# Sparse attention and a top-2 mixture of experts on one core: the eight zero fills of the output at other places in the program

## The chip, the core and the metric

The kernel runs on one core of one Trainium2 chip. The metric is the device time of one execution in microseconds (us), the median of the runs. Five engines work side by side, each with its own queue of instructions: TensorE (PE in the profile; PEld is its weight load), VectorE (DVE), ScalarE (ACT), GpSimd (POOL) and SyncE (SP). SP issues nearly all transfers between the chip's memory (DRAM) and the on-chip memory (SBUF); they run on the core's 16 DMA engines, which all queues share. GpSimd issues the gathers and scatters by row number.

## The reference

Four batches of eight heads, 768 positions, 64 wide. Attention is block-sparse with blocks of 32: a block sees itself, its neighbours, the first and the last block, and three sampled ones; the first and last block see everything.

```
scores = where(mask, q @ k.T / 8, -1e9); attn = softmax(scores); x = attn @ v   # -> 3072 rows of 512
logits = x @ w_gate + log1p(exp(x @ w_noise)) * noise
top2, top2_w = the two largest of 8 experts, softmax over the two
out = zeros((3072, 512)); for e, k: out[rows] += top2_w * (relu(x[rows] @ w1[e]) @ w2[e])
```

The output starts as zeros, since the experts add to it row by row. Those zeros are what the change is about.

## The kernel before, in words

The first part is attention. It is a chain of 64 items, 16 for each batch, walked by `Attention.steps`. Twelve items of a batch are tiles of 128 query rows, `("q", b, t, f)` with tile t of six and half f of the heads; four are the global blocks, `("g", ...)`. Step k writes out the scores of item k+2 (line 264), the transposes of item k (line 331), and the product with the values of item k-1 (line 359), so three items are in work at once. The order of all instructions is the order in which this Python code writes them (`manual_schedule`); each engine takes its own in that order.

SP's queue is filled by the same steps. For a tile it carries q (line 195), the near rows of the values (`va`, line 227) and the three sampled blocks for each 32 rows (`va` and `vb`, line 232). A tile's values come in two halves of seven transfers; in batch four there are two buffers for them instead of three, so that a tile's loads wait until the product of two tiles before has freed its buffer. From the early steps of batches one to three SP also carries the next batch's keys (`kk`, line 172), which GpSimd scales (line 184) and then copies, block by block, to `kc` (lines 204 and 205). Finished rows go to DRAM as `x_rows` (line 636). Each transfer of SP also waits for the completion of the one issued eight places earlier, since eight completion counters are used in turn.

`step(n, 3)` at the end of step n runs what the table `plan` holds for n. Before, this is a memset of `spare()` by GpSimd at step 49 (a part of the buffer `xs[2]`, free by then) and `fill_out(i)` for i = 0 to 7 at steps 49, 50, 51, 52, 54, 55, 56 and 57. One `fill_out` sets 384 rows of the output to zero: a DMA of 768 pieces of 1 KB, 786,432 bytes, out of one zeroed row of 256 floats in each partition. Fills 4 to 7 read the zeroed part of `xg`, which exists from step 53 on. In the same stretch the table loads the first expert's weights (`wraw`, line 905), and from step 59 on gathers the first expert's rows (line 998) and transposes them by DMA (`xta`, line 1008).

The second part are ten units of expert work (lines 1056, 1095, 1142 on TensorE). The first scatter to the output is issued at 352.1 us. After the last unit comes a branch for rows beyond the fixed capacity.

Of the kernel before, what the change touches and what calls it, by code (L numbers as in the profile page):

```python
# [9 lines left out]
F32 = mybir.dt.float32  # L10
# [10 lines left out]
P = 128  # L21
# [7 lines left out]
C = 816  # L29
# [19 lines left out]
class Attention:  # L49
# [25 lines left out]
    def open(self, ctx, early, ident):  # L75
        tc, nc = self.tc, self.nc
        pool = lambda c, name, bufs, **kw: c.enter_context(tc.tile_pool(name=name, bufs=bufs, **kw))
        self.const = pool(ctx, "aconst", 1, side="right")
        self.buf = pool(ctx, "abuf", 1, side="right")
        self.qp = pool(ctx, "aq", 3, side="right")  # L80
        self.pp = pool(ctx, "app", 2, side="right")
        self.gp = pool(early, "agp", 3)
        self.sm = pool(ctx, "asm", 4, side="right")
        self.xp = pool(ctx, "axp", 2, side="right")
        self.ps_s = pool(ctx, "ps_s", 3, space=PSUM)
        self.ps_o = pool(ctx, "ps_o", 2, space=PSUM)
        ep = pool(early, "aeb", 1)
        two = lambda n: ep if n == 2 else self.buf
        J = self.NJ
        self.va = [two(i).tile([P, J, self.HW], F32, name=f"va{i}") for i in range(3)]  # L90
        self.vb = [two(i).tile([P, J, self.HW], F32, name=f"vb{i}") for i in range(3)]
        self.kk = [two(2 - 2 * i).tile([P, self.NB, P], F32, name=f"kk{i}") for i in range(2)]
        self.kc = [self.buf.tile([P, J, self.NP, 8, 32], F32, name=f"kc{i}") for i in range(2)]
        self.qgt = [two(2 - 2 * i).tile([P, self.NP, 64], F32, name=f"qg{i}") for i in range(2)]
        self.ends = [two(2).tile([P, self.HD], F32, name=f"ends{i}") for i in range(2)]
        self.xs = [self.buf.tile([P, self.NP, 2, P], F16, name=f"x{n}") for n in range(2)]
        self.og = self.const.tile([P, 4, self.W], F32, name="og")
        self.known = self.const.tile([P, self.NB, 2], F32, name="known")
        self.pgt = [self.buf.tile([P, 8, P], F32, name=f"pgt{i}") for i in range(4)]
        self.ident = ident  # L100
        self.ident16 = self.const.tile([P, P], F16, name="a_ident16")
        nc.vector.tensor_copy(self.ident16, self.ident)
        nc.vector.memset(self.known, 1.0 / XS)

    def open_x(self, ctx):
        p = ctx.enter_context(self.tc.tile_pool(name="axs", bufs=1))
        self.xs += [p.tile([P, self.NP, 2, P], F16, name=f"x{n}") for n in (2, 3)]
# [1188 lines left out]
def kernel(ctx, tc, qt, qg, kt, vx0, vx1, vx2, vx3, vw, vg, sampled_blocks, gates, noise, w1, w2, out):  # L1296
    nc = tc.nc
# [9 lines left out]
    ex = Experts(tc, router, w1, w2, out, x_dram)  # L1307
    att = Attention(tc, qt, qg, kt, (vx0, vx1, vx2, vx3), vw, vg, sampled_blocks, H, DM // H)
# [16 lines left out]
    PER = NS // att.B  # L1325
    EC = PER * 3 + 5
    UB = 9

    def spare():
        return att.xs[2].rearrange("p n a c -> p (n a c)")[:, 0:512].bitcast(F32)  # L1330

    def fill_out(i):
        z = spare() if i < 4 else ex.xg[:, C // P, 0:512].bitcast(F32)
        nc.sync.dma_start(out[i * 384:(i + 1) * 384].rearrange("(p n) (h d) -> p (n h) d", p=P, d=256),
                          z[:, None, :].to_broadcast([P, 3 * DM // 256, 256]))

    plan = {}
    at = lambda n, f, *a: plan.setdefault(n, []).append((f, a))

    def gather_early(c):  # L1340
        ex.gather(0, c)

    at(PER * 3 + 1, lambda: nc.gpsimd.memset(spare(), 0.0))
    for i in range(8):
        at(PER * 3 + 1 + i + i // 4, fill_out, i)
    for i in range(3):
        at(EC + 1 + i, ex.load_piece, 0, i)
    at(NS - 4, ex.split_piece, 0, 0)
# [162 lines left out]
    for u in range(nu):  # L1511
        left_ = ex.rows(u)[1]
        n = ex.count(u)
# [64 lines left out]
```

## Time and profile before

| what | value |
|---|---|
| median of 3 runs | 862.2 us (859.36 to 864.88) |
| profiled execution | 858.13 us, its span 856.3 us |
| mean granted TensorE clock | 0.964 of full |
| TensorE busy | 793.2 us, 93% of the span |
| attention, first to last product | up to about 312 us |
| DMA traffic | 148.86 MB |

The profile is one execution. A row of the timeline gives the start, the length, the engine, the source line and the operation, and in brackets how long the engine stood idle before it and what ended that. SPq is SP's queue: its length is that of issuing, not of the transfer. In a table of windows the first numbers are the stretch and its length, then the busy time of PE, PEld, DVE, ACT and POOL with the number of instructions, then PEclk (the granted TensorE clock as a share of full), the mean busy share of the DMA engines (it can pass 1 a little) and GB/s.

### The profile page before, as it was taken

The numbers are of one execution on the slowest core, as the hardware profiler recorded it, in microseconds if no ns is written. First come the engines' busy times: TensorE is split into PE (matmuls) and PEld (weight loads), VectorE is DVE, ScalarE is ACT, GpSimd is POOL, SyncE is SP. The second block draws the span as 40 slices with busy tenths as digits, with TensorE's granted clock in tenths as the row PEclk, the third lists the DMA queues.
The fourth block names the chain that finished last, engine by engine and source line by source line (L and its number), as shares of the span: only waits on it lengthen the run. The fifth ranks groups of instructions, "written<-read, shape, count | busy, mean of one in ns | idle before, by whom it ended". The sixth has DMA issues, their size and how long they took to land.

```text
span 856.3 us, 24921 instructions
## 1 busy us (share of the span) xinstructions
PE 793.2 (93%) x9799; PEld 489.4 (57%) x9799; DVE 582.9 (68%) x1160; ACT 400.5 (47%) x736; POOL 380.7 (44%) x656
## 2 busy tenths in 40 slices
PE   7899899988877869999997989999999999999996
PEld 4666576666546647466585544554554554554553
DVE  6765697788687418752528698697697696796631
ACT  5869758858634325322114542552542632633510
POOL 5773587577564230130615426426336335322311
PEclk8999999999978769999999999999999999999999
DMA  7666786685869976650977939639539549523301
GB/s 232 205 189 175 203 234 184 202 237 168 270 192 268 235 182 160 205 181 9 210 169 164 207 122 237 190 100 238 174 111 235 170 115 232 165 90 108 103 29 52
DMA packets 119840, 148.86 MB, mean 174 GB/s; under 512 B 69515, under 2 KB 76300, under 8 KB 119714
## 3 DMA queue, kind: packets, MB, share of 16 engines
q1 hardware_dynamic: 107490, 109.22, 48.3%
q0 software_dynamic: 12224, 37.96, 13.9%
q8 instruction: 79, 1.29, 0.7%
q14 instruction: 47, 0.39, 0.2%
HBM read 107.28 MB, written 26.15 MB: 156 GB/s over the span
## 4 chain that ended last, share of the span: by engine, by line
PE 72%; DVE 10%; DMA 6%; ACT 6%; issue 3%; SPq 2%; POOL 0%; POOLq 0%; DVEq 0%; ACTq 0%
PE pc L1142 28%; PE pa L1095 10%; PE ps L264 5%; PE po L359 5%; PE pd L1095 5%; PE pa L1056 4%; PE ps L331 4%; PE pc L1095 3%; PE pd L1056 2%; PE pc L1151 2%; PE po L382 2%; ACT p L304 2%; DMA va<-in_vx_dram 2%; DVE m L301 2%; DMA va<-in_vw_dram 1%
## 5 line engine op out<-in xcount | busy, mean ns | idle before, releaser
L1142 PE MATMUL pc<-w,hh 128*128 128x512 f16 x768 | 228.4, 379 | 0.0
L1175 POOL DMA_INDIRECT out_dram<-y,r_xT x46 | 64.2, 1395 | 218.4 <-DVE y L1174 179.0
L1095 PEld LDWEIGHTS <-w 128*128 128x128 f16 x1008 | 99.1, 98 | 82.7 <-issue 7.9
L1142 PE MATMUL pc<-w,hl 128*128 128x512 f16 x384 | 145.5, 379 | 0.0
L1142 PEld LDWEIGHTS <-hh 128*128 128x128 f16 x768 | 74.6, 98 | 86.4
L304 ACT ACTIVATE p<-ps,m 128x256 f32<-128x256 f32 x192 | 75.1, 476 | 57.7 <-DVE m L301 51.1
L204 POOL COPY kc<-kk 128x128 f32 x264 | 69.5, 300 | 26.6 <-PE ps L264 19.0
L359 PE MATMUL po<-va,ptr 128*32 128x68 f32 x1536 | 60.7, 235 | 17.4 <-DMA va<-in_vx_dram 9.3
L301 DVE TENSOR_REDUCE m<-ps 128x4 f32<-128x1024 f32 x48 | 58.6, 1221 | 25.1 <-PE ps L264 24.8
L998 POOL DMA_INDIRECT xg<-x_rows,r_xT x46 | 61.5, 1337 | 14.7 <-issue 14.7
L944 DVE SCALAR_TENSOR_TENSOR w<-wraw,w 128x1024 f16<-128x1024 f32 (+1 forms) x58 | 64.2, 1110 | 0.8 <-ACT w L940 0.8
L264 PE MATMUL ps<-kc,q 64*32 64x256 f32 x1536 | 57.4, 408 | 7.4 <-ACT pgt L319 3.1
L1142 PEld LDWEIGHTS <-hl 128*128 128x128 f16 x384 | 37.6, 98 | 45.3
L1016 POOL DMA_INDIRECT pv<-out_dram,r_xT x44 | 49.8, 1132 | 28.5 <-issue 25.0
L359 PE MATMUL po<-vb,ptr 128*32 128x68 f32 x1536 | 58.0, 232 | 2.4 <-issue 1.4
L1095 PE MATMUL pa<-tb,w 128*128 128x408 f16 x288 | 56.6, 340 | 3.8 <-ACT ta L1083 3.8
L359 PEld LDWEIGHTS po<-va,ptr 128*32 128x32 f32 x1536 | 42.3, 114 | 29.6 <-issue 11.0
L940 ACT ACTIVATE w<-wraw 128x1024 f16<-128x1024 f32 (+1 forms) x58 | 55.7, 960 | 5.8 <-DMA wraw<-in_moe_w_dram 5.8
L1095 PE MATMUL pd<-tb,w 128*128 128x408 f16 x288 | 56.5, 336 | 1.9 <-ACT tc L1083 1.9
L1174 DVE SCALAR_TENSOR_TENSOR y<-pc,r_xT,pv 128x512 f32<-128x512 f32 x37 | 27.7, 750 | 43.6 <-PE pc L1142 43.6
L331 PE MATMUL ps<-r_ident,p 128*128 128x128 f32 x384 | 56.5, 292 | 0.5 <-issue 0.5
L1064 ACT ACTIVATE hh<-pa 128x408 f16<-128x408 f32 (+2 forms) x56 | 24.2, 442 | 66.0 <-PE pa L1056 53.9
(239 smaller groups left out, 1544.4 us busy)
## 6 DMA issues: line engine op xcount, KB each, us to landing
wraw<-in_moe_w_dram SPq DMA_DIRECT2D x64, 512.0 KB, 3.9
va<-in_vw_dram SPq DMA_DIRECT2D x40, 384.0 KB, 5.0
vb<-in_vx_dram SPq DMA_DIRECT2D x176, 64.0 KB, 3.6
q<-in_qt_dram SPq DMA_DIRECT2D x24, 256.0 KB, 3.7
va<-in_vx_dram SPq DMA_DIRECT2D x88, 64.0 KB, 4.2
kk<-in_kt_dram SPq DMA_DIRECT2D x18, 256.0 KB, 4.0
x_rows<-x SPq DMA_DIRECT2D x16, 256.0 KB, 3.5
out_dram<-x SPq DMA_DIRECT2D x4, 768.0 KB, 7.3
```

The lines of the kernel that those rows point to most:

```text
L204: nc.gpsimd.tensor_copy(kc[:, j, :, 3 + n], flat[:, bass.ds(self.listed(blk, n), P)].rearrange("p (n c) -> p n c", c=32))
L264: mm = lambda o, l, r: nc.tensor.matmul(o, l, r, start=True, stop=True, skip_group_check=True)
L301: nc.vector.tensor_reduce(m, s.rearrange("p a (e c) -> p a e c", e=2), axis=AX.X, op=ALU.max, negate=True)
L304: i = nc.scalar.activation(p[:, 2 * e + par], s[:, par, 256 * e:256 * e + 256], AF.Exp, bias=m[:, par, e:e + 1])
L331: self.apart(it, par, nc.tensor.transpose(t[:, e, c], p[:, 2 * e + par, P * c:P * c + P], self.ident))
L359: nc.tensor.matmul(o[32 * j:32 * j + 32, h], d[:, h % 2, h // 2, x, 32 * j:32 * j + 32], self.values(v[:, self.slot(t, j)], 4 * f + h), st ...
L940: self.nc.scalar.activation(hi, t, AF.Copy, scale=WS)
L944: self.nc.vector.scalar_tensor_tensor(lo, t, WS, hi, op0=ALU.mult, op1=ALU.subtract)
L998: nc.gpsimd.indirect_dma_start(out=self.xg[0:m, c + self.place(u)], out_offset=None, in_=self.x_dram[0:nr], in_offset=bass.IndirectOffsetO ...
L1095: nc.tensor.matmul(o, w[:, wt, slot, s * P:s * P + P], mv(s, a), start=i == 0 and p in tail, stop=i == 5, skip_group_check=True)
L1142: nc.tensor.matmul(py, h[:, f, o], w(f)[:, x], start=i == 0, stop=i == last)
L1175: d = nc.gpsimd.indirect_dma_start(out=self.out, out_offset=bass.IndirectOffsetOnAxis(ap=r["ix"][0:m, c:c + 1], axis=0), in_=y[0:m], in_of ...
```

## The change

The zeros of fills 0 to 3 come from a tile of their own, `zero`, of 1 KB in each partition, which VectorE sets once at the start; the memset of `spare()` on GpSimd is gone. Fills 0 and 1 move to steps 18 and 27 (batch two), fills 2 and 3 to steps 34 and 43 (batch three). Fills 4 to 7 go from steps 54, 55, 56, 57 to steps 54, 56, 58, 60.

```diff
@@ Attention.open
         nc.vector.memset(self.known, 1.0 / XS)
+        self.zero = self.const.tile([P, 256], F32, name="zero")
+        nc.vector.memset(self.zero, 0.0)
@@ kernel
-    def spare():
-        return att.xs[2].rearrange("p n a c -> p (n a c)")[:, 0:512].bitcast(F32)
-
     def fill_out(i):
-        z = spare() if i < 4 else ex.xg[:, C // P, 0:512].bitcast(F32)
+        z = att.zero if i < 4 else ex.xg[:, C // P, 0:512].bitcast(F32)
@@
-    at(PER * 3 + 1, lambda: nc.gpsimd.memset(spare(), 0.0))
-    for i in range(8):
-        at(PER * 3 + 1 + i + i // 4, fill_out, i)
+    for i in range(4):
+        at(PER * (1 + i // 2) + 9 * (i % 2) + 2, fill_out, i)
+        at(PER * 3 + 6 + 2 * i, fill_out, 4 + i)
```

The order on TensorE and ScalarE stays as it was; VectorE gains one row, GpSimd loses one. What moves is SP's queue. First, its rows at step 18, the start of batch two, where the second tile's values are followed by the next batch's keys, a q tile and two stores; before:

```order
L232 DMA vb_101<-in_vx_dram 32x2048 x2
L172 DMA kk_102<-in_kt_dram 128x512 x2
L195 DMA q<-in_qt_dram 128x512
L636 DMA x_rows<-xe 128x1024 x2
L172 DMA kk_102<-in_kt_dram 128x512
L177 DMA qg_106<-in_qg_dram 128x256
```

and now:

```order
L234 DMA vb_101<-in_vx_dram 32x2048 x2
L174 DMA kk_102<-in_kt_dram 128x512
L1333 DMA out_dram<-zero 768x1x256
L174 DMA kk_102<-in_kt_dram 128x512
L197 DMA q<-in_qt_dram 128x512
L638 DMA x_rows<-xe 128x1024 x2
L174 DMA kk_102<-in_kt_dram 128x512
```

Fill 0 stands between the first and the second load of the keys, ahead of q; fill 2 stands in the same way at step 34, the start of batch three. Fill 1 and fill 3 stand behind the last half of a batch's values, ahead of a q tile or a store.

Second, SP's rows in batch four from the second half of tile 2 to the first half of tile 3; before:

```order
L227 DMA va_96<-in_vw_dram 96x2x512
L232 DMA va_96<-in_vx_dram 32x2048
L232 DMA vb_99<-in_vx_dram 32x2048 x2
L232 DMA va_96<-in_vx_dram 32x2048
L232 DMA vb_99<-in_vx_dram 32x2048 x2
L1334 DMA out_dram<-xg 768x1x256
L905 DMA wraw<-in_moe_w_dram 128x1024
L227 DMA va_97<-in_vw_dram 96x2x512
```

and now:

```order
L229 DMA va_96<-in_vw_dram 96x2x512
L234 DMA va_96<-in_vx_dram 32x2048
L234 DMA vb_99<-in_vx_dram 32x2048 x2
L234 DMA va_96<-in_vx_dram 32x2048
L234 DMA vb_99<-in_vx_dram 32x2048 x2
L907 DMA wraw<-in_moe_w_dram 128x1024
L229 DMA va_97<-in_vw_dram 96x2x512
```

One fill has gone from ahead of tile 3; it comes after that half instead, where the third one stood.

Third, SP's rows at the end of batch four, the two halves of its last tile; before:

```order
L227 DMA va_97<-in_vw_dram 96x2x512
L232 DMA va_97<-in_vx_dram 32x2048
L232 DMA vb_100<-in_vx_dram 32x2048 x2
L232 DMA va_97<-in_vx_dram 32x2048
L232 DMA vb_100<-in_vx_dram 32x2048 x2
L1008 DMA_TRANSPOSE xta<-xg 128x8x128 x2
L227 DMA va_97<-in_vw_dram 96x512
L232 DMA va_97<-in_vx_dram 32x2048
```

and now:

```order
L229 DMA va_97<-in_vw_dram 96x2x512
L234 DMA va_97<-in_vx_dram 32x2048
L234 DMA vb_100<-in_vx_dram 32x2048 x2
L234 DMA va_97<-in_vx_dram 32x2048
L234 DMA vb_100<-in_vx_dram 32x2048 x2
L1333 DMA out_dram<-xg 768x1x256
L1010 DMA_TRANSPOSE xta<-xg 128x8x128 x2
L229 DMA va_97<-in_vw_dram 96x512
L234 DMA va_97<-in_vx_dram 32x2048
```

The eighth fill stands between the two halves of the last tile's values now. Counted along this queue, four fills stand ahead of that last half from the start of batch four's tile 2 on, before and now; ahead of tile 3's second half there were three and are two.

## Rows read from the trace of the kernel before

**Rows 1.** The page's second part: 40 equal slices of 21.4 us, in tenths.

```profile
PEclk8999999999978769999999999999999999999999
DMA  7666786685869976650977939639539549523301
```

**Rows 2.** Windows: stretch, busy time by engine, granted clock, DMA share, GB/s.

```profile
106.00:110.00 4.00, 2.27 (x42) 1.35 (x44) 3.13 (x9) 1.63 (x6) 3.17 (x11) 0.75 1.01 345
...
174.00:178.00 4.00, 2.95 (x98) 2.22 (x98) 2.52 (x8) 2.35 (x8) 4.00 (x16) 1.00 1.01 299
...
132.00:142.00 10.00, 9.66 (x224) 7.02 (x224) 6.58 (x14) 8.71 (x18) 8.23 (x22) 1.00 0.62 191
...
202.00:212.00 10.00, 8.86 (x197) 6.29 (x192) 6.55 (x16) 9.53 (x20) 7.53 (x22) 1.00 0.53 159
226.00:238.00 12.00, 9.18 (x156) 5.91 (x154) 6.52 (x14) 8.18 (x18) 4.30 (x14) 0.86 1.00 335
238.00:246.00 8.00, 4.24 (x133) 3.41 (x127) 7.39 (x35) 2.67 (x7) 6.25 (x18) 0.91 0.22 69
246.00:262.00 16.00, 13.06 (x257) 9.71 (x254) 14.89 (x38) 6.20 (x15) 8.26 (x19) 0.72 0.84 260
262.00:302.00 40.00, 30.52 (x705) 23.18 (x703) 21.92 (x53) 17.50 (x38) 15.13 (x30) 0.83 0.97 247
```

**Rows 3.** SP's timeline where batches two and three begin.

```profile
101.97 1.80 SPq L172 DMA_DIRECT2D kk<-in_kt_dram  x2
103.87 0.37 SPq L195 DMA_DIRECT2D q<-in_qt_dram  x1
...
169.81 1.30 SPq L195 DMA_DIRECT2D q<-in_qt_dram  x1
```

**Rows 4.** Tile q in the stretch 101 to 104.5: from issue to landing.

```profile
DMA to landing us min/median/max: 3.7/3.7/3.7
```

**Rows 5.** GpSimd's timeline at the same places.

```profile
105.56 0.62 POOL L184 TENSOR_SCALAR kk<-kk 128x512 f32<-128x512 f32 x1 [5.37 <-DMA kk<-in_kt_dram]
107.00 0.62 POOL L184 TENSOR_SCALAR kk<-kk 128x512 f32<-128x512 f32 x1 [0.83 <-DMA kk<-in_kt_dram]
...
172.78 1.27 POOL L184 TENSOR_SCALAR kk<-kk 128x512 f32<-128x512 f32 x2 [3.88 <-DMA kk<-in_kt_dram]
```

**Rows 6.** TensorE's timeline at the same places.

```profile
107.73 1.75 PE L264 MATMUL ps<-kc,q 64*32 64x256 f32 x32 [2.58 <-POOL kk L184]
...
174.15 1.10 PE L264 MATMUL ps<-kc,q 64*32 64x256 f32 x32 [0.28 <-ACT p L304]
...
179.07 0.26 PE L359 MATMUL po<-va,ptr 128*32 128x68 f32 x3 [1.76 <-issue]
```

**Rows 7.** The chain that ended last, in batch four: the three longest transfers in it.

```profile
269.05 7.11 DMA va<-in_vx_dram
...
289.46 6.01 DMA va<-in_vw_dram
...
299.06 3.29 DMA vb<-in_vx_dram
```

**Rows 8.** Who waited for whom on TensorE, 215 to 312 us: total, times, longest.

```profile
PE po L359 <- DMA va<-in_vx_dram: 8.5, 4, 3.2
```

**Rows 9.** TensorE's transposes in batch four, ahead of a stall and behind it.

```profile
269.14 1.09 PE L331 MATMUL ps<-r_ident,p 128*128 128x128 f32 x8
...
278.83 1.97 PE L331 MATMUL ps<-r_ident,p 128*128 128x128 f32 x8
```

**Rows 10.** SP's timeline: two fills in batch four.

```profile
249.71 0.55 SPq L1334 DMA_DIRECT2D out_dram<-xg  x1
...
257.80 0.55 SPq L1334 DMA_DIRECT2D out_dram<-xg  x1
```

**Rows 11.** VectorE's timeline: its first wait, and a memset of 256 floats.

```profile
2.00 0.18 DVE L123 CAST rf<-sb 1x72 f32<-1x72 int32 x1 [0.39 <-DMA sb<-in_sampled_blocks_dram]
...
11.96 0.27 DVE L602 MEMSET r_acc<- 128x256 f32 x1
```

## The prediction

> **What bounds the kernel now.** I read the page's slices first, to see where the transfers are dense and where TensorE's clock falls; then windows of the DMA share over the places that a fill leaves or enters; then, at those places, the timelines of SP, GpSimd and TensorE, and the chain.
>
> The slices show two things in the attention part, slices 1 to 15 [rows 1]: the DMA engines are never idle for long, and the only deep dip of TensorE's clock (down to 0.6) lies in slices 12 to 15, about 236 to 321 us, which is the end of batch four. The windows split that up [rows 2]. From 226 to 238 us the engines are full (1.00, 335 GB/s): that is where fills 0 to 3 run. From 238 to 246 they are nearly empty (0.22), because the next values wait for a buffer that TensorE frees. From 246 to 262 they are at 0.84, from 262 to 302 at 0.97. In this last stretch the transfers set the pace: the chain goes through three long ones, 7.11, 6.01 and 3.29 us [rows 7], and TensorE's products with the values wait 8.5 us for them in four stalls [rows 8].
>
> Batches two and three look otherwise: there the chain is work on the engines, with one weak spot each, the start of the batch. At 101.97 SP gets to the next keys late; GpSimd waits 5.37 us for them [rows 3, 5], and TensorE's scores of tile 3 start at 107.73 after 2.58 us of idleness [rows 6]. The row names GpSimd's second scaling, which ended at 107.62; the q tile of these scores was issued at 103.87 and took 3.7 us [rows 3, 4], so it landed at 107.57. Both releasers come from SP's queue at the same spot, and a fill ahead of them delays both.
>
> **The change part by part.** Prices first. One fill is 786,432 bytes. At the 335 GB/s of the stretch in which fills and little else ran it takes 2.35 us, at the 247 GB/s of the full end of batch four 3.2 us [rows 2]; at the 299 GB/s of a full stretch in batch three 2.6 us, which I take, as it is the nearest place. SP issues one in 0.55 us when nothing holds it up [rows 10].
>
> *The new zero tile.* VectorE's memset of 256 floats takes 0.27 us; its first wait, for the sampled blocks, is 0.39 us, and the memset stands ahead of it [rows 11]. Cost 0. GpSimd loses a memset of the same size that nobody waited for: 0.
>
> *Fills 0 to 3 leave batch four.* They ran from 226 to 238 in front of 8 us of nearly idle DMA engines [rows 2], and no engine waits for a transfer there. The next values start when a buffer is free, not when the fills are through. So the gain is 0, and by the same idle stretch it cannot be more than the little that two q tiles behind the fills come earlier.
>
> *Fill 0, step 18.* It stands between the two loads of the keys, ahead of the q tile that tile 3's scores wait for. There is no slack: TensorE idles until that tile is there. Cost 2.6 us; the lower bound is 0, if the fill, which only writes, runs beside the loads, which only read; the upper is 3.2 + 0.55 = 3.75 us. The Trainium skill, "DMA: Bandwidth & Descriptors", section "Queues, rings and completion order", says that on each DMA engine the descriptors of one queue are consumed in ring order. By that rule the q tile waits for the whole fill, as in the value taken, and the lower bound falls away; no row here shows a load that is waited for right behind a fill alone.
>
> *Fill 2, step 34.* The same place in batch three. Here the scores start at 174.15 after 0.28 us of idleness that ended with ScalarE [rows 6]. The q tile was issued from 169.81 to 171.11 [rows 3]; with the 3.7 us of the other one [rows 4], counted from the start of the issue, it landed at 173.5, and at the latest it landed at 174.15. So the slack is at most 0.7 us, and GpSimd waits 3.88 us for the keys as before [rows 5]. Of 2.6 us some 2.2 would come through. But 3 us later TensorE idles 1.76 us for nothing that the profile shows [rows 6], in a window in which the DMA engines are full (1.01) [rows 2]; if what it lacks then arrives during the new stall, part of that goes. I take 1.5, with bounds of 0 and 3.75.
>
> *Fills 1 and 3, steps 27 and 43.* They go to stretches of 10 us in which the DMA engines stand at 0.62 and 0.53, which leaves 3.8 and 4.7 us for 2.6 [rows 2]. Cover: those gaps. Cost 0; without the cover at most the two issues, 1.1 us.
>
> *Fills 4 to 7, later in batch four.* Two effects of opposite sign. Tile 3's second half has one fill less ahead of it, so the first long stall should shrink by up to 2.6 us. But the stall that ends last is that of the last tile's last half (3.29 us of the chain), and ahead of that stand the same four fills, the same values and the same gathers. In a stretch at 0.97 the same bytes take the same time; what is gained early is lost behind the eighth fill. The time that can be won is what the engines were idle: 0.16 of 16 us and 0.03 of 40 us, 2.6 + 1.2 = 3.8 us. What can be lost is a fill that leaves the stretch at 0.84 and is done in the one at 0.97: 2.6 us. I take 0, between the two.
>
> *Sum.* 2.6 + 1.5 + 0 + 0 = 4.1 us. Against the profiled execution: 858.1 + 4.1 = 862.2 us. The median of the runs, 862.2, lies 4.1 above that execution, so the forecast for the median is 862.2 + 4.1 = 866.3 us, say 866. On this kernel about 1%, 8.6 us, is what a measurement can tell from no change; the forecast is half of that.
>
> **The rivals.** *A, faster.* The values of tiles 3 to 5 are late because of what stands ahead of them in the queue, not because of the sum of bytes, and the fills at the batch starts run beside the loads. Then the 3.8 us of idle DMA time in batch four are won and the starts cost some 0 to 2: minus 2 to minus 6 us, about 858. For it: TensorE's stalls of 8.5 us [rows 8] are larger than the whole loss above. Against: 0.97.
>
> *B, nothing.* The fills at the starts cost less than 1 us each, since the stalls there hide in others that follow, and batch four is bound by bytes: within 2 us of 862. For it: the unexplained 1.76 us at 179.07, and that one start has slack. Against: at 107.73 TensorE really waited.
>
> *C, slower by more than 1%.* Place: the two batch starts. Each costs the upper bound, 3.75 us, because the engines are already full behind it (1.01 at 345 GB/s from 106 to 110 us) [rows 2]; the longer stall at 174 us lowers TensorE's clock, after which eight transposes take 1.97 us instead of 1.09 [rows 9], with the scores that follow about 1.6 us; and batch four loses the 2.6 us. Sum 3.75 + 3.75 + 1.6 + 2.6 = 11.7, that is 874. It decides from the point at which the stall at 174.15 grows beyond some 3 us. The Trainium skill, "TensorE: Matmul & The Clock Gate", Part 1, says that the clock is gated by how busy TensorE has been recently; the trace agrees, with a granted clock of 0.72 over 246 to 262 us, where TensorE was busy for 13.06 of 16 us.
>
> **How the numbers follow.** Forecast (plus 2 to plus 7, 864 to 869): 0.42. A: 0.25. B: 0.20. C: 0.13. The predicted time is the forecast's, 866. For 8 in 10 the range runs from 857, which takes in most of A, to 872, which takes in the near half of C. Faster by over 1% (below 853.6) is only A's far end: 0.04. Slower by over 1% (above 870.8) is most of C: 0.11. Within 1%: 0.85.
>
> **What would show each step.** Fill 0: the scores of tile 3 in batch two (first L264 behind the keys' scaling) start after about 5 us of idleness instead of 2.58, and GpSimd waits longer for its second piece of keys. Fill 2: the same scores in batch three start after 2 to 3 us instead of 0.28, and the 1.76 us afterwards is smaller. Fills 1 and 3: the windows around them rise from 0.62 and 0.53 to about 0.85, and no new wait stands behind them. Fills 0 to 3's old place: 226 to 238 us, shifted by the delay, falls from 1.00 to about half, and the first values of tile 2 start no earlier relative to it. Batch four: the first stall of the values shrinks, the last does not, and the time from batch four's first scores to the first expert product stays within 2 us. The forecast is wrong if that time shrinks by more than 3 us (A), or if the starts show no longer stall (B).

## The result, and the profile of the changed kernel

The changed kernel takes 867.7 us (median of 22 runs, 860.5 to 870.5) against 861.3 us of the kernel before (22 runs, 855.5 to 871.5) on the same chip. The ratio is 1.0061, with a 95% interval of 1.0043 to 1.0080: half a per cent slower, some 5.3 us, where the forecast had plus 4.1. (The two medians lie 6.5 us apart, which is inside the interval; the text goes by the ratio.) The profiled execution of the changed kernel took 865.27 us, its span 863.5, against 856.3 before. All line numbers up to the kernel's main function are higher by two now.

The slices of the changed kernel look like those of before [rows 1], apart from slices 11 and 12, about 214 to 259 us, which are emptier now (6 and 3 in the second row, 8 and 6 before):

```profile
PEclk7999999989978969999999989999999999999999
DMA  7765887696638976750978939638639539523301
```

Its windows, with the columns of rows 2: the stretch that takes fill 1, cut as in rows 2; the one that takes fill 3, and batch four, both cut 4 us later than in rows 2, since the same work lies 4 us later there.

```profile
132.00:142.00 10.00, 9.34 (x230) 6.84 (x224) 6.74 (x15) 8.51 (x19) 8.37 (x22) 1.00 0.84 247
206.00:216.00 10.00, 8.79 (x198) 6.30 (x193) 6.48 (x16) 9.46 (x20) 7.56 (x22) 1.00 0.59 191
...
230.00:242.00 12.00, 9.16 (x152) 5.88 (x148) 6.58 (x14) 8.19 (x18) 4.38 (x14) 0.78 0.35 106
242.00:250.00 8.00, 4.80 (x135) 3.76 (x127) 7.16 (x35) 2.68 (x7) 6.27 (x18) 0.91 0.01 2
250.00:266.00 16.00, 12.48 (x254) 8.98 (x249) 15.25 (x38) 6.10 (x15) 8.27 (x19) 0.72 0.79 233
266.00:306.00 40.00, 29.40 (x718) 22.17 (x719) 22.10 (x52) 17.52 (x38) 14.83 (x30) 0.93 1.00 263
```

The old place of fills 0 to 3 fell from 1.00 to 0.35, and the idle stretch behind it is emptier, 0.01 instead of 0.22. The 40 us that end batch four are as full as before: 1.00 instead of 0.97. TensorE's first and last stall for values `va` in batch four, in the kernel before:

```profile
276.29 0.75 PE L359 MATMUL po<-va,ptr 128*32 128x68 f32 x3 [3.22 <-DMA va<-in_vx_dram]
...
301.26 0.31 PE L359 MATMUL po<-va,ptr 128*32 128x68 f32 x4 [1.57 <-DMA va<-in_vx_dram]
```

and in the changed one:

```profile
278.93 0.28 PE L361 MATMUL po<-va,ptr 128*32 128x68 f32 x2 [1.35 <-DMA va<-in_vx_dram]
...
303.57 0.25 PE L361 MATMUL po<-va,ptr 128*32 128x68 f32 x2 [3.50 <-DMA va<-in_vx_dram]
```

The first became shorter and the last longer; one fill less stands ahead of the first now.

Now the two starts. SP's timeline of the changed kernel:

```profile
100.18 0.41 SPq L174 DMA_DIRECT2D kk<-in_kt_dram  x1
100.84 0.65 SPq L1333 DMA_DIRECT2D out_dram<-zero  x1
101.53 0.64 SPq L174 DMA_DIRECT2D kk<-in_kt_dram  x1
102.28 1.82 SPq L197 DMA_DIRECT2D q<-in_qt_dram  x1
...
171.15 0.61 SPq L1333 DMA_DIRECT2D out_dram<-zero  x1
171.81 0.65 SPq L174 DMA_DIRECT2D kk<-in_kt_dram  x1
172.56 0.94 SPq L197 DMA_DIRECT2D q<-in_qt_dram  x1
```

TensorE's timeline at the same places (compare rows 6):

```profile
107.58 1.10 PE L266 MATMUL ps<-kc,q 64*32 64x256 f32 x32 [2.48 <-POOL kk L186]
...
178.97 1.96 PE L266 MATMUL ps<-kc,q 64*32 64x256 f32 x32 [4.67 <-DMA q<-in_qt_dram]
180.86 2.08 PE L384 MATMUL po<-va,pgt 96*64 96x68 f32 x32
```

In this execution batch two starts as before, after 2.48 us of idleness instead of 2.58, for SP had come to the keys 1.8 us earlier (100.18 instead of 101.97). Batch three waits 4.67 us, for the q tile, instead of 0.28, and starts at 178.97 instead of 174.15. The scores after the wait then take 1.96 us instead of 1.10.

GpSimd's second scaling shows the fill at both places. Its keys stand right behind the fill in SP's queue, those of the first scaling ahead of it. It waited 0.83 us at batch two before and ran right behind the first at batch three [rows 5]. In the changed kernel:

```profile
106.89 0.62 POOL L186 TENSOR_SCALAR kk<-kk 128x512 f32<-128x512 f32 x1 [3.23 <-DMA kk<-in_kt_dram]
...
177.42 0.62 POOL L186 TENSOR_SCALAR kk<-kk 128x512 f32<-128x512 f32 x1 [3.12 <-DMA kk<-in_kt_dram]
```

So fill 0 did delay what stands behind it; at TensorE that used up the 1.8 us by which SP was early. The chain of the changed kernel has that q tile in it, and in batch four long transfers as in rows 7:

```profile
172.56 6.27 DMA q<-in_qt_dram
...
272.25 6.37 DMA va<-in_vw_dram
282.51 7.78 DMA va<-in_vw_dram
290.35 5.40 DMA va<-in_vw_dram
...
301.43 4.19 DMA vb<-in_vx_dram
```

One difference lies where the change touches nothing, in the expert part. VectorE waits there 6.74 us (3.81 before) ahead of rows that are transposed by DMA, though the profile names nothing that it waited for, and TensorE then 5.16 us for ScalarE behind it (1.86 before). Timelines of VectorE and of TensorE in the changed kernel:

```profile
497.46 1.01 DVE L959 TENSOR_TENSOR xf<-xtb 128x816 f32<-128x816 f16 x1 [6.74 <-issue]
```

```profile
502.23 2.20 PE L1097 MATMUL pd<-tb,w 128*128 128x408 f16 x6 [5.16 <-ACT tc L1085]
```

### The profile page after: what moved, and what is told of

It is laid out like the page before. It is cut to its first block, busy times and chain, and to the rows that moved or that the text cites. A ratio compares the mean times of both kernels' runs of the same rounds, so it can differ in the third digit from the quotient of the medians.

```text
span 863.5 us, 24922 instructions
## 1 busy us (share of the span) xinstructions
PE 794.6 (92%) x9799; PEld 489.1 (57%) x9799; DVE 584.7 (68%) x1161; ACT 400.9 (46%) x736; POOL 380.8 (44%) x655
## 4 chain that ended last, share of the span: by engine, by line
PE 72%; DVE 9%; DMA 7%; ACT 4%; issue 4%; SPq 3%; POOL 0%; POOLq 0%; DVEq 0%; ACTq 0%
PE pc L1144 28%; PE pa L1097 10%; PE ps L266 6%; PE pd L1097 5%; PE po L361 4%; PE pa L1058 4%; PE ps L333 3%; DMA va<-in_vw_dram 3%; PE pc L1097 2%; PE pd L1058 2%; PE pc L1153 2%; PE po L384 2%; DVE m L303 2%; PE ps L319 1%; ACT p L306 1%
## 5 line engine op out<-in xcount | busy, mean ns | idle before, releaser
L1018 POOL DMA_INDIRECT pv<-out_dram,r_xT x44 | 49.8, 1131 | 28.4 <-issue 24.8
L1066 ACT ACTIVATE hh<-pa 128x408 f16<-128x408 f32 (+2 forms) x56 | 24.1, 443 | 65.2 <-PE pa L1058 49.5
```

## The length of each stretch, in fourteen profiles

One execution is one sample. To see what belongs to the change, I cut every profile at the same ScalarE instructions: those that start first after 100, 132, 166, 194, 223.7, 312, 470 and 520 us in the profile of the kernel before. Since all kernels issue the same 736 ScalarE instructions, a length compares the same work. Lengths in us: the row of the kernel before has the distances of these cuts, and a length in another row is that distance plus what the starts of the same two instructions moved apart. The names of the stretches go by SP's queue, whose rows of step 18 are issued at about 100 us, when TensorE is near tile 3 of batch two. The steps are those of fills 0 to 3 and 4 to 7 (194 to 223.7 takes 29.6 to 29.9 in all but e5, 31.7; 312 to 470 takes 157.4 to 158.3, in e9 to e11 159.5 to 159.8).

| kernel | fills at steps | batch two starts: 100-132 | 132-166 | batch three starts: 166-194 | batch four: 223.7-312 | 470-520 |
|---|---|---|---|---|---|---|
| before | 49 50 51 52, 54 55 56 57 | 32.0 | 34.0 | 28.0 | 88.3 | 50.0 |
| changed | 18 27 34 43, 54 56 58 60 | 32.4 | 34.1 | 31.6 | 87.3 | 54.0 |
| e1 | 18 27 45 43, 54 56 58 60 | 39.6 | 34.9 | 28.4 | 87.7 | 48.5 |
| e2 | 49 50 51 52, 54 55 56 57 | 35.2 | 34.4 | 28.1 | 88.4 | 49.9 |
| e3 | 49 50 51 52, 54 56 58 60 | 33.3 | 34.5 | 29.3 | 88.1 | 53.6 |
| e4 | 18 27 34 43, 54 55 56 57 | 37.9 | 33.7 | 31.6 | 87.8 | 49.5 |
| e5 | 18 27 36 43, 54 56 58 60 | 32.4 | 34.4 | 29.1 | 91.4 | 54.0 |
| e6 | 18 18 34 34, 54 56 58 60 | 37.3 | 33.7 | 30.0 | 84.8 | 49.7 |
| e7 | 27 28 43 45, 54 56 58 60 | 31.6 | 40.0 | 28.5 | 87.5 | 51.0 |
| e8 | 27 28 43 45, 49 50 51 52 | 35.2 | 38.9 | 27.1 | 80.8 | 50.9 |
| e9 | 27 43 49 50, 51 51 52 52 | 33.5 | 33.7 | 29.6 | 78.3 | 50.8 |
| e10 | 18 43 49 50, 51 51 52 52 | 36.3 | 33.7 | 28.0 | 81.0 | 51.7 |
| e11 | 27 34 49 50, 51 51 52 52 | 38.2 | 33.7 | 28.0 | 81.4 | 51.5 |
| e12 | 49 49 50 50, 51 51 52 52 | 32.4 | 35.0 | 29.9 | 83.9 | 51.6 |

The table shows at once that batch two's start varies by more than the change's whole effect where nothing stands there (31.6 to 38.2 us), and that the expert stretch varies from 48.5 to 54.0. The 4 us that the changed kernel's profile lost there cannot be laid to the fills: e4, with the same first four, took 49.5, and of the six kernels with the last four at 54, 56, 58 and 60 three took about 54 and three 48.5 to 51.0. That the three long ones are all among these six is not explained.

## The experiments

Theory 1 was that the loss is made at the batch starts, where a q tile waits behind a whole fill in SP's queue. The rivals: the bytes cost the same anywhere in batches two and three (theory 2); the last four fills, the expert part (theory 3) or the new tile make it. All edits but e2's and e3's are to the changed kernel (e3's is to e2, so it has the zero tile); the diffs write its steps out as a list. Each ratio is to the kernel before on the same chip.

**e1, fill 2 alone moved away.**

```diff
-(18, 27, 34, 43, 54, 56, 58, 60)
+(18, 27, 45, 43, 54, 56, 58, 60)
```

> The changed kernel with fill 2 alone moved, from the start of batch three (step 34) to step 45, behind the values of the next batch's first tile. Theory 1 (the q tile behind fill 2 in SP's queue): the scores of tile 3 in batch three start without the 4.67 us stall, some 4 us of the loss come back, ratio to the kernel before 1.000 to 1.002. Theory 2 (the same bytes cost the same wherever they stand in batch three): the loss stays, 1.005 to 1.007. Theory 3 (the loss comes from the last four fills or from the expert part, not from the starts): it stays too, 1.005 to 1.007, but then without any stall at this place.

864.4 us, ratio 1.0027 [0.9990, 1.0064]. The start of batch three took 28.4 us, as before. But the start of batch two, with fill 0, took 39.6 us in this profile. The ratio came between the theories, and its interval takes in both.

**e2, the zero tile alone.** The kernel before, with fills 0 to 3 out of `zero`.

```diff
-        z = spare() if i < 4 else ex.xg[:, C // P, 0:512].bitcast(F32)
+        z = att.zero if i < 4 else ex.xg[:, C // P, 0:512].bitcast(F32)
```

> The kernel before with the zero tile alone: fills 0 to 3 read the new tile, the memset on GpSimd is gone, all eight fills stand at their old steps. Theory 1 and my prediction (tile costs 0): ratio 0.999 to 1.001. Rival (the new tile shifts the other buffers or the program, and the 4 us that the expert part took longer come from that): 1.003 to 1.006.

861.6 us, 1.0013 [0.9983, 1.0042]: no cost that can be told from none.

**e3, the last four alone moved.**

```diff
-(49, 50, 51, 52, 54, 55, 56, 57)
+(49, 50, 51, 52, 54, 56, 58, 60)
```

> Fills 4 to 7 at their new steps 54, 56, 58, 60; fills 0 to 3 at their old steps 49 to 52 (out of the new zero tile). Theory 1 (the loss is made at the starts of batches two and three; batch four gives about 1 us back): ratio to the kernel before 0.998 to 1.001, stretch of batch three's start 28 us as before. Rival (the last four make the loss): 1.004 to 1.007.

861.0 us, 1.0018 [0.9985, 1.0052]; batch four 88.1 us instead of 88.3. The other order in batch four is worth nothing, as predicted. The small excess in the profile lies in the expert stretch (53.6).

**e4, the first four alone moved.**

```diff
-(18, 27, 34, 43, 54, 56, 58, 60)
+(18, 27, 34, 43, 54, 55, 56, 57)
```

> The changed kernel with fills 4 to 7 back at steps 54 to 57, so only fills 0 to 3 are moved. Theory 1 (fill 2 at a batch's start makes the loss, batch four gives about 1 us back): 1.006 to 1.008, a little above the changed kernel. Theory 3 (the later fills 6 and 7 make the loss): 1.000 to 1.002.

865.9 us, 1.0069 [1.0039, 1.0099]: the whole loss, without the last four. Both starts wait in its profile. TensorE's timeline:

```profile
109.50 1.96 PE L266 MATMUL ps<-kc,q 64*32 64x256 f32 x32 [5.62 <-POOL kk L186]
...
183.89 1.96 PE L266 MATMUL ps<-kc,q 64*32 64x256 f32 x32 [5.79 <-DMA q<-in_qt_dram]
```

e2, e3 and e4 together leave the first four's places as the likely cause; theory 3 and the tile explain none of it that these intervals show, though the intervals, up to 1.0052 and 1.0042, leave room for a part.

**e5, fill 2 behind the q tile.**

```diff
-(18, 27, 34, 43, 54, 56, 58, 60)
+(18, 27, 36, 43, 54, 56, 58, 60)
```

> The changed kernel with fill 2 two items later (step 36): the same bytes in the same stretch of batch three, but behind the q tile and two stores in SP's queue instead of ahead of them. Theory 1 (order in the queue): scores of tile 3 in batch three start on time, 1.000 to 1.003. Theory 2 (bytes in a full stretch): a stall of 2 to 4 us shows within the next 10 us, 1.004 to 1.007.

866.8 us, 1.0062 [1.0026, 1.0097]. The scores of tile 3 start after 0.62 us, and the stretch takes 29.1 us, but 194 to 223.7 takes 2 us more, with a wait of 1.14 us for `vb`, and batch four 91.4 (3.1 more). The total speaks for theory 2, the place where it was lost does not: it is spread over 120 us behind, and one profile cannot tell how much of that belongs to the fill. Inconclusive.

**e6, two fills at each start.**

```diff
-(18, 27, 34, 43, 54, 56, 58, 60)
+(18, 18, 34, 34, 54, 56, 58, 60)
```

> The changed kernel with fills 1 and 3 moved to the batch starts too: two fills between the keys at step 18 and two at step 34. Theory 1 (what waits there waits for the whole transfer of each fill, about 2.6 us): the stretch of batch three's start grows from 31.6 us to about 34, that of batch two's start by about as much, in all some 5 us above the changed kernel, ratio 1.010 to 1.013. Rival (a fill there costs a fixed hold-up, or the starts only happened to be long): as the changed kernel, 1.005 to 1.007.

866.8 us, 1.0082 [1.0049, 1.0116], less than expected; the interval takes in the rival's 1.005 to 1.007 and part of theory 1's range. Here the landing shows the price. SP's timeline, and under it the landing of the q tile issued there:

```profile
101.73 0.41 SPq L174 DMA_DIRECT2D kk<-in_kt_dram  x1
102.19 2.01 SPq L1333 DMA_DIRECT2D out_dram<-zero  x2
104.25 1.40 SPq L174 DMA_DIRECT2D kk<-in_kt_dram  x1
105.76 1.15 SPq L197 DMA_DIRECT2D q<-in_qt_dram  x1
```

```profile
DMA to landing us min/median/max: 6.1/6.1/6.1
```

The q tile landed at 111.8, 10.1 us after the first keys' issue. With one fill it was 7.3 (e4), 7.9 (e1) and 8.8 (e5). Without one it was 5.4 (e7), 5.6 (before), 5.9 (e3), 6.1 (e2) and 7.3 (e11). Means 6.1, 8.0, 10.1: about 2 us for each fill ahead in the queue. The values are in the SP and q rows of those profiles; e11's landing is taken from the end of TensorE's wait for it, and the other five traces hold no landing of this tile.

All fourteen profiles have GpSimd's two scalings, whose keys stand ahead of the fill and right behind it. The second of e6, at batch two and at batch three:

```profile
111.27 0.62 POOL L186 TENSOR_SCALAR kk<-kk 128x512 f32<-128x512 f32 x1 [5.70 <-DMA kk<-in_kt_dram]
...
181.37 0.62 POOL L186 TENSOR_SCALAR kk<-kk 128x512 f32<-128x512 f32 x1 [5.46 <-DMA kk<-in_kt_dram]
```

How much later the second scaling starts than the first, and how long TensorE idles before the scores of tile 3, in us (range, mean, number of profiles; the fill of e5 at step 36 stands behind both pieces of keys and counts as none):

| fills between | second scaling, batch two | second scaling, batch three | TensorE, batch two | TensorE, batch three |
|---|---|---|---|---|
| none | 0.6 to 1.7, 1.1 (8) | 0.6 to 2.1, 1.1 (10) | 0 to 4.1, 2.0 | 0 to 0.6, 0.2 |
| one | 3.5 to 4.7, 4.0 (5) | 3.3 to 4.4, 3.8 (3) | 2.5 to 5.6, 4.1 | 1.9 to 5.8, 4.1 |
| two | 6.3 (1) | 6.1 (1) | 6.3 | 2.3 |

So each fill delays the keys behind it by 2.3 to 2.9 us, at both places, and the ranges do not overlap. How much of that reaches TensorE depends on what slack the execution has. In the length of batch three's stretch the dose does not show: 30.0 us with two fills, 31.6, 31.6 and 28.0 with one (changed, e4, e11).

**e7, both starts left free.**

```diff
-(18, 27, 34, 43, 54, 56, 58, 60)
+(27, 28, 43, 45, 54, 56, 58, 60)
```

> The changed kernel with fills 0 and 2 away from the batch starts, behind fills 1 and 3 in the quieter middle (steps 27, 28, 43, 45). Theory 1: both starts as in the kernel before, ratio 0.998 to 1.002. Theory 2 (786,432 bytes more in batches two and three cost the same anywhere): 1.004 to 1.007.

863.5 us, 1.0038 [1.0008, 1.0069], nearer to theory 2's range than to theory 1's. Both starts are as before, but the stretch in between takes 40.0 us instead of 34.0. SP's timeline and TensorE's show why:

```profile
143.82 0.58 SPq L1333 DMA_DIRECT2D out_dram<-zero  x1
144.45 0.63 SPq L229 DMA_DIRECT2D va<-in_vw_dram  x1
145.18 1.01 SPq L234 DMA_DIRECT2D va<-in_vx_dram  x1
```

```profile
152.07 0.86 PE L361 MATMUL po<-va,ptr 128*32 128x68 f32 x3 [3.05 <-DMA va<-in_vx_dram]
...
154.78 1.94 PE L319 MATMUL ps<-r_ident,pg 128*96 128x128 f32 x8
```

The fill of step 28 stands ahead of the values that TensorE needs next: it waits 3.05 us, and eight transposes behind the wait take 1.94 us instead of 1.04 elsewhere in this profile. The DMA engines stood at 0.54 from 140 to 148 us, with the fill's begin in it. A low share of the stretch is no cover by itself; here what stands right behind the fill decided. This is theory 1 at a place that was not chosen for it. e8, with a fill at the same step, waits 3.19 us at the same place.

**e8, nothing left in the late part of batch four.** All fills out of `zero`.

```diff
-(18, 27, 34, 43, 54, 56, 58, 60)
+(27, 28, 43, 45, 49, 50, 51, 52)
```

> All eight fills out of the zero tile: four in the quiet middles (steps 27, 28, 43, 45) and four at steps 49 to 52, ahead of the stretch of batch four in which the DMA engines are nearly idle; none is left in the later part of batch four. If batch four's late part is bound by the sum of its bytes (my prediction), four fills less, about 10 us of DMA time at 0.97, take most of the 8.5 us of stalls away: 4 to 8 us faster than the kernel before, ratio 0.991 to 0.995. Rival (the values there wait for buffers or for one long transfer each, not for the bytes ahead): 0.998 to 1.002.

858.5 us, 0.9965 [0.9932, 0.9999]: less than expected, for the loss of step 28 is in it (38.9 us in the table). Batch four takes 80.8 us instead of 88.3, 7.5 less, where 4 to 8 had been forecast for the whole.

**e9, six fills in the idle stretch.** As e8, but:

```diff
-(27, 28, 43, 45, 49, 50, 51, 52)
+(27, 43, 49, 50, 51, 51, 52, 52)
```

> All fills out of the zero tile: one behind the next batch's first half tile in batches two and three (steps 27 and 43, where the changed kernel's fills 1 and 3 cost nothing), six at steps 49 to 52, ahead of the nearly idle stretch of batch four; none at a batch start, none in batch four's later part, and the second fill at step 28, behind which the values of the next batch waited, is gone. Theory 1 with batch four bound by its bytes: starts as before, batch four 80 to 82 us instead of 88.3, some 7 to 10 us faster than before, ratio 0.988 to 0.992. Rival (six fills reach into the next values and give the gain back): 0.995 to 1.000.

854.4 us (8 runs), 0.9895 [0.9859, 0.9932]: 9.1 us faster than the kernel before (0.0105 of 863.1), the lowest of all, though the intervals of e11 and e12 overlap its own. Windows of this kernel, with the columns of rows 2 and cut at the same times; the work lies 2.6 us later here:

```profile
238.00:246.00 8.00, 6.68 (x141) 4.30 (x140) 5.51 (x30) 3.21 (x10) 5.07 (x17) 0.73 1.05 359
246.00:262.00 16.00, 11.65 (x245) 8.49 (x248) 15.53 (x43) 6.76 (x17) 9.56 (x21) 0.81 0.80 233
262.00:302.00 40.00, 32.18 (x880) 24.62 (x870) 24.23 (x62) 18.29 (x40) 16.11 (x31) 0.99 0.91 226
```

and who waited for whom on TensorE, 215 to 312 us (8.5 us before [rows 8]):

```profile
PE po L361 <- DMA va<-in_vx_dram: 2.2, 2, 1.4
```

The stretch that was idle is full (1.05 instead of 0.22), the late part is a little less full (0.91 instead of 0.97; 0.95 if cut 2.6 us later), TensorE's clock there is 0.99 instead of 0.83, and the stalls for these values are down from 8.5 to 2.2 us (3.3 and 3.6 in e10 and e11, with the same six fills there).

**e10 and e11, one fill of e9 at a start.**

```diff
-(27, 43, 49, 50, 51, 51, 52, 52)
+(18, 43, 49, 50, 51, 51, 52, 52)
```

```diff
-(27, 43, 49, 50, 51, 51, 52, 52)
+(27, 34, 49, 50, 51, 51, 52, 52)
```

> The kernel with six fills in the idle stretch, its first fill at step 18 (start of batch two) instead of step 27, nothing else changed. Theory 1: the fill at the start costs what the q tile's landing is delayed by in the profiles so far, 2.2 us (5.8 us behind the first keys without a fill, 8.0 with one), less what slack there is: ratio 0.002 to 0.003 above the same kernel without it. Rival (batch two's start varies as much without a fill, 31.6 to 35.2 us, and a fill adds nothing on average): equal.

> The kernel with six fills in the idle stretch, its second fill at step 34 (start of batch three) instead of step 43. Theory 1: the stretch of batch three's start takes 31.6 us instead of 28.2 as in the changed kernel, ratio 0.003 to 0.005 above the same kernel without it. Rival (the 3.4 us were chance, as the doubled fills with 30.0 us suggest): below 0.002.

e10: 858.9 us, 0.9963 [0.9929, 0.9997]; e11: 857.5 us, 0.9922 [0.9892, 0.9952]. Against e9's median that is 4.6 us for the fill at step 18, more than theory 1 had, and 3.1 us for that at step 34, about its lower end. The interval of e10 hardly meets that of e9, that of e11 overlaps it. e9, e10 and e11 carry the same bytes in each batch, so theory 2 would have the three equal. In e11's profile the start of batch three took 28.0 us, with a wait of 1.91 us. Its start of batch two, without a fill, took 38.2, with a wait of 4.10 us.

**e12, all eight there.**

```diff
-(27, 43, 49, 50, 51, 51, 52, 52)
+(49, 49, 50, 50, 51, 51, 52, 52)
```

> All eight fills at steps 49 to 52, none anywhere else. They need 18.8 us at 335 GB/s from 226 us on, so they end at about 245 us, where the idle stretch ends. Theory (the idle stretch holds them all): as with six there, 0.987 to 0.992. Rival (the last two reach into the values of tile 2, or hold up the q tile behind them): 2 to 5 us slower than with six, 0.992 to 0.996.

857.5 us (11 runs), 0.9912 [0.9876, 0.9948]. Its interval covers that of e9 for the most part; batch four takes 83.9 us in its profile instead of 78.3, but e10 and e11, with six fills there, took 81.0 and 81.4. Whether two fills more are too many there is not told apart from chance.

## Why the prediction came out right, and where it did not

*The sum.* Plus 4.1 was forecast, plus 5.3 measured. e4 against e2 and e3 puts most of the loss at the first four fills, and e9 against e10 and e11 at the two starts among them. The means over the profiles below give 1.8 and 1.9 us for the two starts, 3.7 together, the two pairs of runs 4.6 and 3.1, 7.7 together; the total measured lies between. Rival B (nothing) is outside the interval, and so is C (slower by more than 1%).

*Fill 0, +2.6.* The mechanism and the price hold: with one fill ahead, the keys behind it come 2.9 us later on the mean at batch two and 2.8 at batch three, and the q tile lands about 2 us later for each fill, so the lower bound of 0 (a fill beside the loads) falls away. The Trainium skill, "DMA: Bandwidth & Descriptors", section "Queues, rings and completion order", had ring order for that, and the landings of e6 agree (the fills at 107.1 and 110.2 us, the keys at 111.2, the q tile at 111.8, in the order of issue). The forecast's second sign, GpSimd's longer wait for its second piece of keys, showed in the changed kernel itself (3.23 us instead of 0.83). But its first sign, 5 us of idleness, did not show in the changed kernel (2.48) nor in e5 (2.92); it showed in e1 (4.67), e4 (5.62) and e10 (4.56), and nearly in e11 (4.10), which has no fill there. The start took 35.7 us on the mean of the five profiles with one fill, 33.9 on that of the eight without: plus 1.8, with single values some 7 us apart on either side. The pair e9 and e10 gives 4.6. So the price in the queue was right, and that 2.6 us is also what TensorE loses is known only within this scatter.

*Fill 2, +1.5.* Mis-sized in the profile at hand: 31.6 against 28.0, plus 3.6. The forecast let 1.1 us (of 2.6) go in slack and in the unexplained idleness at 179.07; that idleness did vanish, but the wait was 4.67 us. I had left out that the scores behind a long wait run slower (1.96 instead of 1.10 us), which only rival C had in its sum. (C let that begin beyond a stall of some 3 us; in e12 the scores of tile 3 in batch two took 1.96 us behind a wait of 2.44, in the changed kernel 1.10 behind one of 2.48. Its 0.72 of clock from 246 to 262 us comes behind 8 us in which TensorE was busy for 4.24 [rows 2].) Over the profiles the mean is 30.4 with one fill (31.6, 31.6, 28.0) and 28.5 without (nine; e5 left out), plus 1.9, so 1.5 was no bad mean; the pair e9 and e11 gives 3.1. Against all this stands e5, where the wait is gone (0.62 us) and nothing of the total came back.

*Fills 1 and 3, 0.* Right: 34.1 and 29.7 us in their stretches, as before. The window of fill 1 rose to 0.84, as I said, that of fill 3 only to 0.59; but the reason given, room in the window, was not enough. e7 shows that a fill one step later, in a window at 0.54, costs 6 us, for values stand behind it.

*Fills 0 to 3 out of batch four, 0.* Right: 87.3, 87.7, 87.8 and 87.5 us in four of the kernels without them there, 88.3 before; 91.4 and 84.8 in e5 and e6.

*Fills 4 to 7 later, 0.* Right (e3), and as far as the runs show for the reason given: from batch four's first scores (203.14 us before, 207.14 now) to the first expert product it is 111.3 us instead of 112.2, and the bytes ahead of the end are the same. The first stall shrank (3.22 to 1.35 us) and the last did not (1.57 to 3.50), as forecast; over the profiles this is weaker, with a first stall of 3.0 to 3.9 us in three with the old order of the last four and 1.4 to 3.9 in six with the new one, and a last one of 1.6 to 3.0 and 2.1 to 4.0. The end moved clearly only when bytes left. Four fills less in the late part are worth 7.5 us of the 10.4 that they need at 2.6 each (e8). Rival A, which had order and not bytes, falls. What A had right is that time lies in those stalls; the change did not touch it.

*Open.* Why batch two's start varies by 6 us without a fill, why VectorE waits 2 to 7 us ahead of the transposed rows in the expert part, and whether the fill at step 36 (e5) costs anything. These were seen, not explained.

## What to carry to other kernels

A transfer that nobody waits for is paid by the first one behind it in the same queue that somebody waits for: choose its place by what stands behind it, not by the mean share of the stretch. Where the end of a stage is bound by bytes, another order of the same bytes is worth nothing; take bytes out, to where the DMA engines idle because the next load waits for a buffer. And where runs of one kernel differ by more than the effect, compare the same stretch over several profiles before a stall in one of them is called the cause.

## What the runs showed of the hardware that I had not expected

Fourteen profiles of almost the same program agree within 0.3 us from 194 to 223.7 us (but for one) and within 0.4 us in the 300 us behind 520, but differ by 6 to 8 us at one batch start, where SP comes to the keys at 98.8 to 102.5 us and TensorE mostly has no slack. So the run-to-run spread of the kernel before, 855 to 871 us on one chip, probably comes from a few places where the queue is only just in time; with one profile of each kernel this is argued, not shown. In the idle stretch the fills and a q tile moved at 359 GB/s (e9), more than the 335 of the kernel before. And a load that stands in SP's queue right behind a fill comes later by about the time that a fill takes, 2.3 to 2.9 us for each. In fourteen profiles the values with none, one and two fills ahead do not overlap, while the length of the same stretch scatters by more than that.
